# Queries and keys loaded with rows twice, low parts of probabilities in one operation a tile later, value blocks moved by 64

## The chip, the cores and the metric

The kernel runs on one core of a Trainium2 chip. The metric is the device time of one execution in microseconds (us). Before the change it is 1229.49 us, the median of three runs (1227.45 to 1229.86).

## What is computed

Attention with a threshold, then two feed-forward blocks, cut here to the arithmetic:

```python
# q, k, v: (4, 8, 576, 64), float32; tau = 0.02
scores = q @ k.T / 8
scores = where(scores >= rowmax(scores) - tau, scores, -1e9)
attn = exp(scores - rowmax(scores)); attn = attn / sum(attn)
x = (attn @ v).transpose(0, 2, 1, 3).reshape(2304, 512)
x = (silu(x @ w_gate) * (x @ w_val)) @ w_out      # 512 -> 1536 -> 512
x = (relu(x @ w_in) ** 2) @ w_out2                # 512 -> 2048 -> 512
```

All of it is float32; the weights reach the chip as 64-bit numbers. To keep the accuracy the kernel splits operands into a high part (rounded to the type in which PE multiplies) and a low part (the rest).

## The kernel before

**Tiles.** Attention is cut into 144 tiles of 128 query rows by 576 keys: 4 batches x 4 pairs of heads (NPAIR = 4) x 9 tiles. Of a pair's nine, A0 to A3 are the first head's rows 0 to 511, T is the last 64 rows of both heads together, and B2, B3, B0, B1 are the second head's. Tiles 0 to 35 are batch 0, tile 36 is the first of batch 1.

**A tile.** QK (L667, on PE) makes scores with the operands `qs` (rows 0 to 63 the high part of the scaled, transposed query, rows 64 to 127 its low part), `kh` (the high keys twice, one copy under the other) and `kl` (the low keys twice): two matmuls for each half of the columns give all four products of high and low. For tile T the operand is `qt`, in which the last 64 queries of each head have their own columns. RED (L677, DVE) takes the row maximum and subtracts tau, CUT (L685, ACT) applies the threshold, EXP (L693, ACT) the exponential with its row sum, RCP (L698, DVE) the reciprocal `r`. Then the two ways part:

- Batch 0: NORM on POOL, transposes on PE, copies `PH` on ACT and DVE, and value matmuls at L773.
- Batches 1 to 3 ("VV"): NORM on POOL makes `rs` (L706, one column, r times a constant) and the rounded high part of the probabilities in f16 (L707, into a buffer `both`). LO (L755, DVE) makes the low part, e x rs minus the high part, in two operations of 512 and 64 columns. XT (L761, a DMA on the SP queue) transposes high and low together, 9 blocks of 128 columns, into `pt`. AV (L780, PE) collects the tiles of one part of a head (there are four parts a pair, PARTS) and multiplies 14 times: 5 blocks of high probabilities and 4 of low ones by the high values `vs`, 5 blocks of high probabilities by the low values `v3`. The 576 high columns fill four blocks and a half, so the low ones begin in the middle of block 4: LO writes its last 64 columns there and its first 512 in blocks 5 to 8, and both use the same blocks of `vs`. ACT (L789) and DVE take the result out of PSUM.

**Preparing a pair.** `pair_steps` is a list of steps, one a tile, that runs through the tiles of the pair before. One load (`load_pair`, L472, SP queue) brings queries, keys and values of both heads, one head on rows 0 to 63, the other on 64 to 127, into `raw`, which has one buffer. Then come the rounded query (L612, ACT, into `land`), rounded keys (L70, ACT), low query (L618, DVE) and low keys (L78, POOL, two operations of 288 columns). `move` (L602) then copies each of the three to the rows where QK needs it, twice, by six SBUF-to-SBUF DMAs of half height a head on the SP queue. `tail` (L74, POOL) copies the last 64 queries into `qt`; for the T tile `kd` (L606) and `qd` (L608) are moved too. `values` splits the head's values out of the same `raw`: two copies (L74) and two subtractions, all on POOL. So `raw` is read until the next pair's own steps begin, and the next pair's load waits for the last reader.

**Fill.** Between tiles PE also works on the first feed-forward block for finished batches (`fill_group`: L258 and L300 matmuls); a credit in columns (`rate` 2600 a tile) sets how much. From about 541 us on the rest of the feed-forward blocks runs alone.

**Order.** The program names the steps in the order of the loop over `i` (the tile index): RED, CUT, EXP of tile i, then RCP, NORM, LO and XT of tile i - 1, QK of tile i + 1, fill, value matmuls of tiles `late` = 5 back, a step of `pair_steps`. A scheduler then orders each engine's instructions, with offsets (`early0`, `early`) that lift or lower steps. The engines and the SP queue run theirs strictly in order, and an instruction waits for semaphores at its place in the row.

```python
    both = [es[-1].bitcast(F16)[:, : 2 * S], *(ptp.tile(...) for j in range(2))]
            if i - 1 >= 9 * NPAIR:
                at_(LO, i - 1)
                at_(XT, i - 1)
```

The first line is of note: one of the three `both` buffers is the storage of the third `e` buffer, so in batches 1 to 3 EXP alternates between two.

Of the kernel before, what the change touches and what calls it, by code (L numbers as in the profile page):

```python
# [84 lines left out]
def attention_moe(tc, qkv, qk0, tau, w1, w2, out, cfg):  # L85
# [423 lines left out]

    def values(hd, h, raw):  # L510
# [11 lines left out]
        ops.sub(cfg["vl"], hd["v3"][:, :, :D], v, v2)  # L522

    def first_pair():

        raw = load_pair(0)
        for h in range(2):
            r = raw if h == 0 else rawp.tile([P, 2 * S], F32, name="raw01", tag="land")
            if h:
                for c in (0, S):  # L530
                    nc.sync.dma_start(r[:, c : c + S], qk0[h, :, c : c + S])
            else:

                for c in (slice(0, P), slice(S, 2 * S), slice(P, S)):
                    nc.sync.dma_start(r[:, c], qk0[h, :, c])
# [50 lines left out]
    def pair_steps(p):  # L586

        raw = load_pair(p)
        land = rawp.tile([P, 2, S], F32R, name=f"land{p}", tag="land")
        q, k = raw[:, 0:S], raw[:, S : 2 * S]  # L590
        qh, kh = land[:, 0], land[:, 1]

        def move(h):
            hd = head(h)
            rows = slice(hd["odd"] * D, (hd["odd"] + 1) * D)
            for dst, parts_ in (
                (hd["qs"], (qh, q.bitcast(F32R))),
                (hd["kh"], (kh, kh)),
                (hd["kl"], (k.bitcast(F32R), k.bitcast(F32R))),
            ):  # L600
                for j, src in enumerate(parts_):
                    nc.sync.dma_start(dst[j * D : (j + 1) * D, :].bitcast(F32), src[rows, :].bitcast(F32))  # L602
            tail(hd)
            if not hd["odd"]:
                hd["qd"], hd["kd"] = qds[0], qp.tile([P, S], F32R, name=f"kd{p}", tag="kd", bufs=1)
                nc.sync.dma_start(hd["kd"].bitcast(F32), k)  # L606
                for c in (slice(0, D), slice(D, P)):
                    nc.sync.dma_start(hd["qd"][c, c].bitcast(F32), qh[c, 4 * P : S].bitcast(F32))  # L608
# [1115 lines left out]
```

## Time and profile before

| | |
|---|---|
| median of 3 runs | 1229.49 us |
| the profiled execution, device time | 1229.54 us |
| its span in the trace | 1227.8 us |
| mean granted clock of TensorE | 0.968 |
| PE busy | 1113.4 us (91%), 6194 matmuls |
| DVE busy | 887.3 us (72%) |
| ACT busy | 615.1 us (50%) |
| POOL busy | 307.8 us (25%) |
| HBM read, written | 93.06 MB, 22.28 MB |

PE is TensorE's matmuls, PEld its weight loads, DVE VectorE, ACT ScalarE, POOL GpSimd, SP SyncE, whose queue (SPq) issues DMAs. Shares of busy time are of the whole span; attention with its fill takes the first 540 us, so a stage has to be looked at by itself. The granted clock is the share of TensorE's full 2.4 GHz that the chip allowed.

### The profile page before, as it was taken

The page shows a single profiled execution, that of the slowest core. Times are in us where ns is not written, and L with a number is a line of the kernel's source. Part 1 is how long each engine was busy: PE and PEld are TensorE (multiplying, and loading weights), DVE is VectorE, ACT ScalarE, POOL GpSimd, SP SyncE. Part 2 cuts the span into 40 slices and gives each one's busy share as a digit, 9 for nine tenths or more (in the row PEclk, how much of TensorE's full clock was granted, in tenths as well). Part 3 has the DMA queues.
Part 4 walks back from the last instruction along what each step waited for, and adds up shares of the span by engine and source line. Part 5 has one row for each costly group of instructions (what it writes and reads, how often), then busy time and mean ns, then how long its engine had stood idle before and what let it go on. Part 6 is the DMA issues. An engine that isn't in the chain of part 4 may idle for free.

```text
span 1227.8 us, 18958 instructions
## 1 busy us (share of the span) xinstructions
PE 1113.4 (91%) x6194; PEld 965.7 (79%) x6194; DVE 887.3 (72%) x2088; ACT 615.1 (50%) x1377; POOL 307.8 (25%) x524
## 2 busy tenths in 40 slices
PE   7998877667878877899999999999999999999998
PEld 6776766456667765799888888889889899889997
DVE  7888865765676757659998687878765858867554
ACT  7886644455554545535543343434555545554232
POOL 5577755654555646310000000000000000000000
PEclk9999988789989899999999999999999999999999
DMA  7768867777897787613222013436435444544452
GB/s 209 217 180 201 192 137 157 142 162 160 166 174 169 154 164 159 127 36 99 89 80 85 17 44 120 146 118 223 184 147 185 166 155 158 183 155 151 177 182 92
DMA packets 188258, 179.90 MB, mean 147 GB/s; under 512 B 138112, under 2 KB 139392, under 8 KB 188160
## 3 DMA queue, kind: packets, MB, share of 16 engines
q1 hardware_dynamic: 188016, 178.70, 54.4%
q8 instruction: 49, 0.80, 0.3%
q14 instruction: 49, 0.40, 0.1%
q10 hardware_dynamic: 144, 0.00, 0.0%
HBM read 93.06 MB, written 22.28 MB: 94 GB/s over the span
## 4 chain that ended last, share of the span: by engine, by line
PE 55%; POOL 14%; issue 9%; DMA 8%; DVE 8%; SPq 3%; ACT 3%; POOLq 0%; DVEq 0%; ACTq 0%
PE mm L258 16%; PE mm L1532 15%; PE mm L1479 11%; PE mm L300 7%; DMA raw<-in_qkv_dram 3%; POOL both L707 3%; POOL raw L78 3%; PE bank L258 2%; DMA qs<-raw 2%; POOL e L707 2%; DMA wr<-in_w_dram 2%; PE bank L780 1%; POOL vs L74 1%; POOL rs L706 1%; DVE st__114 L677 1%
## 5 line engine op out<-in xcount | busy, mean ns | idle before, releaser
L677 DVE TENSOR_SCALAR_CACHE_REDUCE st__114<-s,tau_c 128x576 bf16<-128x576 f32 x144 | 116.7, 811 | 36.8 <-PE s L667 25.9
L685 ACT ACTIVATE z<-s,thr 128x576 f32<-128x576 f32 x144 | 106.3, 738 | 48.9 <-DVE st__114 L677 40.6
L693 ACT ACTIVATE e<-z 128x577 f32<-128x577 f32 x144 | 98.5, 684 | 60.0 <-DVE r L698 38.8
L258 PE MATMUL mm<-xs,wa 128*128 128x512 f32 (+2 forms) x672 | 125.7, 347 | 0.5 <-ACT x L70 0.5
L258 PEld LDWEIGHTS mm<-xs,wa 128*128 128x128 f32 x672 | 109.4, 188 | 15.7 <-ACT x L70 0.7
L258 PE MATMUL bank<-xs_m,wa 128*128 128x288 f32 x576 | 100.2, 316 | 19.4 <-DVE xs_m L78 11.6
L780 PE MATMUL bank<-pt,vs 128*128 128x256 f16 (+1 forms) x432 | 76.5, 321 | 40.7 <-DMA pt<-both 21.2
L755 DVE SCALAR_TENSOR_TENSOR both<-e,rs,both 128x512 f16<-128x512 f32 (+1 forms) x144 | 85.6, 635 | 37.5 <-POOL both L707 37.2
L667 PE MATMUL s<-kh,qs 128*128 128x288 f32 x256 | 88.0, 361 | 24.9 <-ACT z L685 14.3
L258 PEld LDWEIGHTS bank<-xs_m,wa 128*128 128x128 f32 x576 | 86.2, 200 | 25.7 <-DVE xs_m L78 13.9
L780 PEld LDWEIGHTS <-vs 128*128 128x128 bf16 x432 | 41.2, 107 | 61.9 <-issue 28.4
L667 PEld LDWEIGHTS s<-kh,qs 128*128 128x128 f32 x256 | 50.5, 200 | 41.4 <-ACT z L685 26.0
L667 PE MATMUL s<-kl,qs 128*128 128x288 f32 x256 | 74.6, 312 | 3.7 <-DMA kl<-raw 3.7
L258 PE MATMUL mm<-xs,wb 128*128 128x512 f32 (+1 forms) x360 | 74.9, 368 | 0.0
L1549 DVE TENSOR_TENSOR xF<-xF,mm 128x512 f32<-128x512 f32 x54 | 36.9, 684 | 51.0 <-PE mm L1532 50.9
L258 PEld LDWEIGHTS mm<-xs,wb 128*128 128x128 f32 x360 | 62.8, 188 | 11.3
L755 DVE SCALAR_TENSOR_TENSOR e<-e,rs,e 128x512 f16<-128x512 f32 x72 | 47.2, 696 | 29.9 <-POOL e L707 29.8
L1532 PE MATMUL mm<-wb,wx 128*128 128x512 f32 x270 | 67.2, 389 | 0.0
L70 ACT ACTIVATE wb<-wf 128x256 fp32r<-128x256 f32 x82 | 34.0, 414 | 65.5 <-DVE wf L1134 38.4
L1479 PE MATMUL mm<-right,wb 128*128 128x384 f32 x348 | 65.3, 335 | 0.8 <-DVE right L78 0.8
L1131 ACT ACTIVATE wf<-wr 128x256 f32<-128x256 f32 x64 | 27.6, 433 | 69.6 <-DMA wr<-in_w_dram 49.3
L1479 PEld LDWEIGHTS mm<-right,wb 128*128 128x128 f32 x348 | 60.8, 188 | 1.5 <-DVE right L78 1.0
(163 smaller groups left out, 2645.7 us busy)
## 6 DMA issues: line engine op xcount, KB each, us to landing
wr<-in_w_dram SPq DMA_DIRECT2D x106, 256.0 KB, 3.0
raw<-in_qkv_dram SPq DMA_DIRECT2D x15, 896.0 KB, 5.9
kh<-land SPq DMA_DIRECT2D x60, 144.0 KB, 2.7
kl<-raw SPq DMA_DIRECT2D x60, 144.0 KB, 2.9
xF<-in_w_dram SPq DMA_DIRECT2D x30, 256.0 KB, 3.2
right<-kept1T SPq DMA_DIRECT2D x8, 768.0 KB, 5.5
right<-kept0T SPq DMA_DIRECT2D x7, 768.0 KB, 5.4
right<-kept SPq DMA_DIRECT2D x6, 768.0 KB, 4.3
```

Of the source, the lines that this page charges most:

```text
L258: mm(pt[:, :n], w[:, a, col + c * P : col + (c + 1) * P], xs[:, b, c, :], start=(i == 0), stop=(i == len(TERMS) - 1),)
L300: mm(pt[:, :n], ws[k][:, a, 2 * DM + m * P : 2 * DM + (m + 1) * P], us[k][:, b, :], start=(k == 0 and i == 0), stop=(k == ahead and i == 2),)
L667: mm(sp[:, cols], l, r[:, cols], start=(n_ == 0), stop=(n_ == len(pairs) - 1),)
L677: red = nc.vector.tensor_scalar(st_, st[t]["s"][:, :S], scalar1=tau_c, scalar2=None, op0=ALU.subtract, op1=ALU.max, accum_out=th)
L685: nc.scalar.activation(z[:, :S], st[t]["s"][:, :S], AF.Prelu, bias=st[t]["thr"], scale=-1.0, alpha=1 / SLOPE)
L693: ex = nc.scalar.activation(e, st[t]["z"], AF.Exp, scale=-SLOPE, accum_out=sum_)
L707: norm = nc.gpsimd.tensor_scalar(a[:, :S], e, scalar1=rs, scalar2=1.0, op0=ALU.mult, op1=ALU.mult)
L755: nc.vector.scalar_tensor_tensor(a[:, to : to + c.stop - c.start], e[:, c], r, a[:, c], op0=ALU.mult, op1=ALU.subtract)
L780: mm(o[:, :n], v, pt[:, k if k < 9 else k - 9, lo : lo + n], start=(k == 0), stop=(k == 13))
L1479: mm(bank[:, :BK], w[:, a, c * P : (c + 1) * P], t[:, b, c, :], start=(n == 0 and x in ("11", "12", "S1")), stop=(n == 5), skip_group_chec ...
L1532: mm(pt, u[:, b, s * P : (s + 1) * P], w[a], start=(half == 0 and j == 0 and i == 0), stop=(half == 1 and j == 1 and i == 2),)
L1549: nc.vector.tensor_tensor(acc[:, j, :], acc[:, j, :], pt, op=ALU.add)
```

## The change

**Queries and keys.** The input now holds each head's queries and keys with its 64 rows twice, so one load a head (`raw_head`, 128 x 1152, two buffers) lands them on all 128 rows. The rounded query and keys are computed at their place in `qs` and `kh`, the low query (64 rows) and the low keys too. `move`, `land`, `kd` and `qd` are gone. A pair has two query operations instead of one (on ACT; on POOL for pairs 1 to 3), two of keys (ACT), two low queries of 64 rows (DVE), four low-key operations (POOL) instead of two.

**Values.** They have a load of their own (`value_steps`): a pair's values are fetched at the seventh tile of the pair before and split at the pair's own tiles 3 and 5, the two copies on ACT instead of POOL. `vs` and `v3` have two buffers instead of three.

**Low parts.** LO is one operation of 576 columns that starts in the middle of block 4 and runs on, so the four low blocks hold keys shifted by 64 against the high ones. A second copy of the values, `vb`, shifted by 64 rows in the same way, is made of `vs` by two DMAs a head. LO and XT are issued one tile later, value matmuls too (`late` 6), `both` has three buffers of its own, and `rs` moves from POOL to DVE.

**Tile T** takes four pairs of factors (8 matmuls) instead of three (6).

```diff
@@ both, v3s, loads
-    both = [es[-1].bitcast(F16)[:, : 2 * S], *(ptp.tile([P, 2 * S], F16, name=f"both{j}", tag=f"both{j}") for j in range(2))]
-    v3s = [ptp.tile([P, 5, P], BF16, name=f"v3{j}", tag=f"v3{j}") for j in range(3)]
+    both = [ptp.tile([P, 2 * S], F16, name=f"both{j}", tag=f"both{j}") for j in range(3)]
+    v3s = [ptp.tile([P, 5, P], BF16, name=f"v3{j}", tag=f"v3{j}") for j in range(2)]
...
-    def load_pair(p):
-        raw = rawp.tile([P, RAWW], F32, name=f"raw{p}", tag="raw")
-        if p:
-            nc.sync.dma_start(raw, qkv[p])
-        return raw
+    def raw_head(h):
+        return rawp.tile([P, 2 * S], F32, name=f"raw{h}", tag=f"raw{h % 2}")
@@ values
-        vs = hd["vs"] = qp.tile([P, 5, P], BF16, name=f"vs{h}", tag="vs", bufs=3)
+        vs = hd["vs"] = qp.tile([P, 5, P], BF16, name=f"vs{h}", tag="vs", bufs=2)
...
         ops.sub(cfg["vl"], hd["v3"][:, :, :D], v, v2)
+        hd["vb"] = qp.tile([P, 4, P], BF16, name=f"vb{h}", tag="vb", bufs=2)
+        nc.sync.dma_start(hd["vb"][:D], vs[D:, :4])
+        nc.sync.dma_start(hd["vb"][D:], vs[:D, 1:])
@@ pair_steps (the old body is printed above)
+        raws = [raw_head(2 * p + j) for j in range(2)]
+
+        def query(j):
+            hd, q = head(2 * p + j), raws[j][:, :S]
+            if p < NPAIR:
+                nc.gpsimd.tensor_scalar(hd["qs"], q, scalar1=qscale, scalar2=1.0, op0=ALU.mult, op1=ALU.mult)
+            else:
+                nc.scalar.activation(hd["qs"], q, AF.Copy, scale=qscale)
+
+        def key(j):
+            hd, q = heads[2 * p + j], raws[j][:, :S]
+            ops.copy(cfg["kh"], hd["kh"], raws[j][:, S:])
+            low = hd["qs"][D:, :]
+            nc.vector.scalar_tensor_tensor(
+                low, q[D:, :], qscale[D:, :], low.bitcast(F32), op0=ALU.mult, op1=ALU.subtract
+            )
+
+        def key_low(j, c):
+            hd = heads[2 * p + j]
+            ops.sub(cfg["kl"], hd["kl"][:, c], raws[j][:, S:][:, c], hd["kh"][:, c].bitcast(F32))
+
+        halves_ = (slice(0, HS), slice(HS, S))
+        nc.sync.dma_start(raws[0], qk[2 * p])
         yield None
+        nc.sync.dma_start(raws[1], qk[2 * p + 1])
         yield None
+        query(0)
         yield None
+        key(0)
         yield None
+        key_low(0, halves_[0])
         yield None
+        key_low(0, halves_[1])
+        tail(heads[2 * p])
         yield None
+        if p < NPAIR:
+            values(heads[2 * p], 2 * p)
+        query(1)
         yield "next"
+        key(1)
+        key_low(1, halves_[0])
         yield None
+        key_low(1, halves_[1])
+        tail(heads[2 * p + 1])
+        if p < NPAIR:
+            values(heads[2 * p + 1], 2 * p + 1)
         yield None
+
+    def value_steps(i):
+        p, k = divmod(i, 9)
+        if k == 6 and NPAIR <= p + 1 < B * NPAIR:
+            rawv[p + 1] = rawp.tile([P, 2 * VW], F32, name=f"rawv{p + 1}", tag="rawv")
+            nc.sync.dma_start(rawv[p + 1], values_[p + 1])
+        if k in (3, 5) and NPAIR <= p < B * NPAIR:
+            h = 2 * p + (k == 5)
+            values(heads[h], h, rawv[p])
@@ QK, EXP, RCP, LO, AV
-            pairs = [(hd["qt"][:], hd[x_]) for hd in (ha, hb) for x_ in ("kh", "kl") if x_ == "kh" or "kd" not in ha]
-            if "kd" in ha:
-                pairs.append((ha["qd"], ha["kd"]))
+            pairs = [(hd["qt"][:], hd[x_]) for hd in (ha, hb) for x_ in ("kh", "kl")]
...
-        e = es[t % (len(es) if t < 9 * NPAIR else len(es) - 1)]
+        e = es[t % len(es)]
...
+        if way(t) == "VV":
+            rs = st[t]["rs"] = sm.tile([P, 1], F32, name=f"rs{t}", tag="rs")
+            nc.vector.tensor_scalar(rs, r, scalar1=UNIT, scalar2=None, op0=ALU.mult)
...
-        for to, c in ((S + D, slice(0, 4 * P)), (S, slice(4 * P, S))):
-            nc.vector.scalar_tensor_tensor(
-                a[:, to : to + c.stop - c.start], e[:, c], r, a[:, c], op0=ALU.mult, op1=ALU.subtract
-            )
+        nc.vector.scalar_tensor_tensor(a[:, S:], e[:, :S], r, a[:, :S], op0=ALU.mult, op1=ALU.subtract)
...
-                v = hd["vs"][:, (0, 1, 2, 3, 4, 0, 1, 2, 3)[k], :] if k < 9 else hd["v3"][:, k - 9, :]
+                v = hd["vs"][:, k, :] if k < 5 else hd["vb"][:, k - 5, :] if k < 9 else hd["v3"][:, k - 9, :]
@@ the loop over i
-            if i - 1 >= 9 * NPAIR:
-                at_(LO, i - 1)
-                at_(XT, i - 1)
+        if 9 * NPAIR <= i - 2 < NTILE:
+            at_(LO, i - 2)
+            at_(XT, i - 2)
...
+            at_(value_steps, i, name="PS")
@@ the input and CFG
+    q, k = (x.reshape(B * H, S, D).transpose(0, 2, 1) for x in (q, k))
+    qk = np.concatenate([np.concatenate([x, x], axis=1) for x in (q, k)], axis=2)
...
-    full[NPAIR:, D:, :, 4] = full[NPAIR:, :D, :, 4]
+    full[NPAIR:, D:, :, 4] = full[NPAIR:, :D, :, 0]
...
-    "vh": "P",
+    "vh": "A",
-    "late": 5,
+    "late": 6,
```

**How the order moves.** First the SP queue at the end of batch 2, where pair 11's queries and keys are moved and pair 12's are loaded. Before (`raw_3423` and `land_3425` belong to pair 11, `qs_3711` and so on to its second head, `raw_3791` is pair 12's load):

```order
L606 DMA kd_3625<-raw_3423 128x576
L608 DMA qd_136<-land_3425 64x64 x2
L761 DMA_TRANSPOSE pt<-e_104 128x9x128
L602 DMA qs_3711<-land_3425 64x576
L602 DMA qs_3711<-raw_3423 64x576
L602 DMA kh_3712<-land_3425 64x576 x2
L602 DMA kl_3713<-raw_3423 64x576
L761 DMA_TRANSPOSE pt<-both_106 128x9x128
L602 DMA kl_3713<-raw_3423 64x576
L761 DMA_TRANSPOSE pt<-both_107 128x9x128
L761 DMA_TRANSPOSE pt<-e_104 128x9x128
L472 DMA raw_3791<-in_qkv_dram 128x1792
```

The same queue in the changed kernel (`raw_3293` is the load of pair 11's second head, `raw_3662` that of pair 12's first, `vs` and `vb` are values of pair 10):

```order
L609 DMA raw_3293<-in_qk_dram 128x1152
L768 DMA_TRANSPOSE pt<-both_108 128x9x128
L768 DMA_TRANSPOSE pt<-both_106 128x9x128
L768 DMA_TRANSPOSE pt<-both_107 128x9x128
L519 DMA vb_3348<-vs_3343 64x512
L520 DMA vb_3348<-vs_3343 64x512
L768 DMA_TRANSPOSE pt<-both_108 128x9x128
L607 DMA raw_3662<-in_qk_dram 128x1152
L768 DMA_TRANSPOSE pt<-both_106 128x9x128
L768 DMA_TRANSPOSE pt<-both_107 128x9x128
```

Between the transposes there are only loads and the two copies into `vb`; no row of the queue waits for ACT, DVE or POOL to have split queries or keys.

Second, ACT at the head of the program: the first keys, the first query, then CUT (L685 before, L693 after) and EXP (L693, L701) of tiles 0 and 1. Before:

```order
L70 ACTIVATE kh_150<-raw_142 128x288 x2
L571 ACTIVATE qs_149<-raw_142,qscale 128x448
L685 ACTIVATE z_105<-s_121,thr_166 128x576
L693 ACTIVATE e_102,sum_169<-z_105 128x577
L685 ACTIVATE z_105<-s_122,thr_175 128x576
```

After:

```order
L69 ACTIVATE kh_148<-raw_140 128x288 x2
L568 ACTIVATE qs_147<-raw_140,qscale 128x448
L69 ACTIVATE vs_1214<-rawv_1038 128x5x64
L69 ACTIVATE vs_1306<-rawv_1038 128x5x64
L693 ACTIVATE z_105<-s_120,thr_164 128x576
L69 ACTIVATE vs_1214<-rawv_1038 128x5x64
L701 ACTIVATE e_102,sum_167<-z_105 128x577
L69 ACTIVATE vs_1306<-rawv_1038 128x5x64
L693 ACTIVATE z_105<-s_121,thr_173 128x576
```

The four copies of pair 4's values (used from tile 36 on) stand among the first two tiles' operations.

Third, DVE in the middle of the attention stage: RED (L677 before, L685 after), LO (L755, L764), RCP (L698, L706) and, after, `rs` (L709) and the low query (L598). Before:

```order
L698 RECIPROCAL r_3384<-sum_3343 128x1
L677 TENSOR_SCALAR st__114,thr_3426<-s_122,tau_c 128x576
L755 SCALAR_TENSOR_TENSOR both_107<-e_103,rs_3386,both_107 128x512
L755 SCALAR_TENSOR_TENSOR both_107<-e_103,rs_3386,both_107 128x64
L698 RECIPROCAL r_3433<-sum_3381 128x1
L677 TENSOR_SCALAR st__114,thr_3465<-s_121,tau_c 128x576
L755 SCALAR_TENSOR_TENSOR e_104<-e_102,rs_3435,e_104 128x512
L755 SCALAR_TENSOR_TENSOR e_104<-e_102,rs_3435,e_104 128x64
```

After:

```order
L685 TENSOR_SCALAR st__113,thr_3295<-s_121,tau_c 128x576
L764 SCALAR_TENSOR_TENSOR both_108<-e_103,rs_3267,both_108 128x576
L706 RECIPROCAL r_3301<-sum_3263 128x1
L598 SCALAR_TENSOR_TENSOR qs_3387<-raw_3292,qscale,qs_3387 64x576
L709 TENSOR_SCALAR rs_3303<-r_3301 128x1
...
L685 TENSOR_SCALAR st__113,thr_3352<-s_120,tau_c 128x576
L764 SCALAR_TENSOR_TENSOR both_106<-e_104,rs_3303,both_106 128x576
```

A tile's LO stands one RED behind its RCP before and after alike (`r_3384`, `thr_3426`, LO with `rs_3386`; `r_3301`, `thr_3352`, LO with `rs_3303`); what is new in the row is `rs` on DVE and one operation in the place of two.

## Rows read from the trace of the kernel before

**Rows 1.** Busy us by stretch: PE, PEld, DVE, ACT, POOL (count), clock, DMA share, GB/s

```profile
27.00:91.83 64.83, 59.80 (x360) 50.97 (x359) 55.12 (x147) 56.34 (x131) 40.83 (x58) 1.00 0.71 197
91.83:492.57 400.74, 308.14 (x1920) 253.61 (x1919) 279.47 (x656) 209.60 (x470) 234.99 (x397) 0.90 0.80 164
541.10:1200.00 658.90, 657.22 (x3378) 582.97 (x3379) 494.50 (x1142) 300.43 (x669) 0.00 (x0) 1.00 0.40 137
500.00:513.00 13.00, 10.46 (x71) 8.55 (x72) 10.18 (x29) 9.60 (x21) 5.50 (x13) 1.00 0.77 138
```

**Rows 2.** Timeline of DVE, line 677: start, duration, operation, [wait and releaser]

```profile
91.83 0.81 DVE L677 TENSOR_SCALAR_CACHE_REDUCE st__114<-s,tau_c 128x576 bf16<-128x576 f32 x1
...
269.29 0.82 DVE L677 TENSOR_SCALAR_CACHE_REDUCE st__114<-s,tau_c 128x576 bf16<-128x576 f32 x1
...
284.53 0.82 DVE L677 TENSOR_SCALAR_CACHE_REDUCE st__114<-s,tau_c 128x576 bf16<-128x576 f32 x1 [5.13 <-PE s L667]
...
289.20 0.82 DVE L677 TENSOR_SCALAR_CACHE_REDUCE st__114<-s,tau_c 128x576 bf16<-128x576 f32 x1 [0.70 <-ACT e L693]
...
291.30 0.82 DVE L677 TENSOR_SCALAR_CACHE_REDUCE st__114<-s,tau_c 128x576 bf16<-128x576 f32 x1 [0.34 <-issue]
...
492.57 0.82 DVE L677 TENSOR_SCALAR_CACHE_REDUCE st__114<-s,tau_c 128x576 bf16<-128x576 f32 x1 [0.66 <-PE s L667]
```

**Rows 3.** Timeline of POOL and of the SP queue at tiles 80 and 81

```profile
267.10 2.01 POOL L78 TENSOR_TENSOR raw<-raw,land 128x288 fp32r<-128x288 f32 x2
...
280.18 1.26 SPq L602 DMA_DIRECT2D kl<-raw  x2
...
287.84 0.24 POOL L74 TENSOR_SCALAR qt<-qs 128x64 fp32r<-128x64 f32 x1 [9.11 <-DMA qs<-raw]
...
292.41 0.47 SPq L472 DMA_DIRECT2D raw<-in_qkv_dram  x1
```

**Rows 4.** Waits, 91.83 to 492.57: waiter <- releaser: us in all, times, longest

```profile
ACT xF L789 <- PE bank L780: 54.7, 22, 8.4
POOL qt L74 <- DMA qs<-raw: 45.7, 8, 9.1
```

**Rows 5.** Groups by form, 91.83 to 492.57: busy us, mean ns | idle before

```profile
L755 DVE SCALAR_TENSOR_TENSOR both<-e,rs,both 128x512 f16<-128x512 f32 x66 | 56.6, 857 | 34.5 <-POOL both L707 34.2
L755 DVE SCALAR_TENSOR_TENSOR both<-e,rs,both 128x64 f16<-128x64 f32 x66 | 28.0, 424 | 0.0
L74 POOL TENSOR_SCALAR vs<-raw 128x320 bf16<-128x320 f32 x44 | 23.0, 523 | 14.3 <-DMA raw<-in_qkv_dram 12.2 <-PE bank L780 1.1
L698 DVE RECIPROCAL r<-sum 128x1 f32<-128x1 f32 x100 | 15.5, 155 | 3.2 <-ACT e L693 3.0
L618 DVE SCALAR_TENSOR_TENSOR raw<-raw,qscale,land 128x576 fp32r<-128x576 f32 x11 | 10.8, 980 | 4.1 <-ACT land L612 4.1
L612 ACT ACTIVATE land<-raw,qscale 128x576 fp32r<-128x576 f32 x11 | 8.5, 773 | 7.7 <-DMA raw<-in_qkv_dram 7.0 <-issue 0.6
```

**Rows 6.** A dense run of PE in the chain that ended last: start, us, releaser

```profile
521.41 11.20 PE bank L258 x84
```

**Rows 7.** Start of the program: timeline of SP queue and ACT, then DMA issues

```profile
7.23 0.33 SPq L472 DMA_DIRECT2D raw<-in_qkv_dram  x1
...
8.07 0.74 ACT L685 ACTIVATE z<-s,thr 128x576 f32<-128x576 f32 x1 [2.43 <-DVE st__114 L677]
...
raw<-in_qkv_dram SPq DMA_DIRECT2D x15, 896.0 KB, 5.9
x<-in_qkv_dram SPq DMA_DIRECT2D x8, 160.0 KB, 3.5
```

**Rows 8.** Timeline of DVE: LO while POOL subtracts low keys, and later

```profile
267.17 2.02 DVE L755 SCALAR_TENSOR_TENSOR e<-e,rs,e 128x512 f16<-128x512 f32 x2 [0.62 <-POOL e L707]
...
289.95 0.94 DVE L755 SCALAR_TENSOR_TENSOR both<-e,rs,both 128x512 f16<-128x512 f32 x2
```

More of the change, by code (lines that the diff above doesn't have):

```diff
@@ L82, in split, with attention_moe @@
         self.sub(elo, lo, src, hi.bitcast(F32))
-def attention_moe(tc, qkv, qk0, tau, w1, w2, out, cfg):
+def attention_moe(tc, qk, values_, tau, w1, w2, out, cfg):
     nc = tc.nc
@@ L506, in whole_values, with values @@
             c0 += hd["odd"] * D
-            a = 2 * S + hd["odd"] * VW
-            nc.sync.dma_start(flat[:, c0 : c0 + VW], qkv[h // 2, :, a : a + VW])
-    def values(hd, h, raw):
+            a = hd["odd"] * VW
+            nc.sync.dma_start(flat[:, c0 : c0 + VW], values_[h // 2, :, a : a + VW])
+    def values(hd, h, raw=None):
         odd = hd["odd"]
@@ L522, in values @@
         ops.sub(cfg["vl"], hd["v3"][:, :, :D], v, v2)
+        hd["vb"] = qp.tile([P, 4, P], BF16, name=f"vb{h}", tag="vb", bufs=2)
+        nc.sync.dma_start(hd["vb"][:D], vs[D:, :4])
+        nc.sync.dma_start(hd["vb"][D:], vs[:D, 1:])
     def first_pair():
[L526 removed]
         for h in range(2):
[L528 removed]
+            r = raw_head(h)
             if h:
                 for c in (0, S):
[L531 removed]
+                    nc.sync.dma_start(r[:, c : c + S], qk[h, :, c : c + S])
             else:
                 for c in (slice(0, P), slice(S, 2 * S), slice(P, S)):
[L535 removed]
+                    nc.sync.dma_start(r[:, c], qk[h, :, c])
                 nc.vector.tensor_scalar(qscale, tau_t, scalar1=0.0, scalar2=0.125, op0=ALU.is_ge, op1=ALU.mult)
@@ L579, in s2 @@
                 tail(hd)
-                values(hd, h, raw)
+                values(hd, h)
             yield s0
@@ L586, in pair_steps @@
     def pair_steps(p):
[L588 to L608, printed above, removed]
+        raws = [raw_head(2 * p + j) for j in range(2)]
@@ L625, in pair_steps @@
-        move(2 * p)
+        key_low(0, halves_[1])
+        tail(heads[2 * p])
         yield None
-        values(heads[2 * p], 2 * p, raw)
+        if p < NPAIR:
+            values(heads[2 * p], 2 * p)
+        query(1)
         yield "next"
-        move(2 * p + 1)
+        key(1)
+        key_low(1, halves_[0])
         yield None
-        values(heads[2 * p + 1], 2 * p + 1, raw)
+        key_low(1, halves_[1])
+        tail(heads[2 * p + 1])
+        if p < NPAIR:
+            values(heads[2 * p + 1], 2 * p + 1)
@@ L704, in NORM @@
             a = st[t]["both"] = both[(t + 1) % len(both)]
-            rs = st[t]["rs"] = sm.tile([P, 1], F32, name=f"rs{t}", tag="rs")
-            nc.gpsimd.tensor_scalar(rs, r, scalar1=UNIT, scalar2=1.0, op0=ALU.mult, op1=ALU.mult)
+            rs = st[t]["rs"]
             norm = nc.gpsimd.tensor_scalar(a[:, :S], e, scalar1=rs, scalar2=1.0, op0=ALU.mult, op1=ALU.mult)
@@ L951, in attention_moe @@
             at_(av_parts, 3, name="AV")
-        if i == 4:
-            with tc.issue_after(st[2]["norm"]):
-                for x_ in qds:
-                    nc.gpsimd.memset(x_.bitcast(F32), 0.0)
         at_(mp1.flush, "P", name="FP")
@@ L1657, in pack @@
     return [
-        ("in_qkv_dram", np.ascontiguousarray(qkv)),
-        ("in_qk0_dram", np.stack([np.concatenate([qkv[0, r : r + D, : 2 * S]] * 2) for r in (0, D)])),
+        ("in_qk_dram", np.ascontiguousarray(qk)),
+        ("in_v_dram", full.reshape(B * NPAIR, P, 2 * VW)),
         ("in_tau_dram", np.ascontiguousarray(tau)),
```

23 lines of the change are left out of this document (4 added, 19 removed).

## The prediction

> **What bounds the kernel now.** I read the stages first, from the busy time by stretch [rows 1]. Its columns give, for each engine, busy microseconds, and then granted clock and share of the DMA engines. From 541 us on PE has hardly a gap (657 of 659 us up to 1200), and the change touches nothing there. Tiles 0 to 35 (batch 0) end at 91.8 us; from 27 us on PE is busy 92% of the time (59.80 of 64.83), DVE 85%, ACT 87%. The weak stretch lies between the row maxima of tile 36 (91.83) and tile 135 (492.57): 400.74 us for eleven head pairs, **36.4 us a pair**, with PE at 77%, DVE at 70%, and a granted clock of 0.90, so part of it ran at the lower of the two levels.
>
> Next, the rhythm in it: the times of L677, the first operation of a tile on DVE [rows 2]. Within a pair tiles follow each other every 2.2 us or so (289.20 to 291.30), but tile 81, the first of a pair, starts at 284.53 after DVE had stood idle for QK's matmuls; the tile before it had started at 269.29. From pair 6 to pair 15 the step to a pair's first tile is 9.8 to 22.2 us, ten of ten. Eight steps of 2.2 us make 17.6 of the 36.4; the rest is the boundary.
>
> Then the cause, from the waits and the SP queue. At that boundary POOL had the low keys ready at 269.1; SP moved them to their rows at 280.18, behind the transposes in its queue, and moved the odd head's after them; POOL itself stood 9.11 us at `tail` for moved queries, with the NORMs of the next tiles behind it; and the next pair's load went out only at 292.41, since its one buffer had to be read out first [rows 3]. Over the stretch POOL lost 45.7 us to those query moves, and ACT 54.7 us to value matmuls that came late [rows 4]. So the boundary is a serial chain, load, split, move, QK, across four engines and one queue.
>
> **The change, part by part.**
>
> *Moves and the late load.* Twelve half-height moves, kd and two qd a pair go. In the new SP order no step of the query and key path stands on SP but the two loads, and these stand some nine tiles ahead of the operations that read them. The chain of the boundary then has no transfer left in it, and a pair costs what its busiest engine needs. So I price a pair by each engine, from the eleven-pair sums [rows 1] and durations of one operation [rows 5].
>
> - PE: 1920 recorded matmuls, 174.5 a pair, plus 2 (a T tile now has four pairs of factors instead of three). Dense, 84 of them took 11.20 us, 0.133 each [rows 6], so 176.5 x 0.133 = 23.5 us. At batch 0's 92% that is 25.6. At the busy time it has now, 28.0 + 0.3 over 0.92, it is 30.8: that would be with the clock no better than 0.90.
> - DVE: 279.47/11 = 25.4 us. LO's two operations take 857 + 424 = 1.28 us a tile; the one of 576 columns is nearest to L618 (two f32 inputs, 576 columns, mean 0.98), so 9 x 0.30 = 2.7 us go. `rs` comes over from POOL: 9 x 0.155 = 1.4 (price of L698, also one column). The low queries are 2 x 0.98 instead of one: +1.0. Together 25.1 us. At batch 0's 85% this is **29.5 us**; at PE's 92% it would be 27.3.
> - ACT: 209.60/11 = 19.1 us, plus one query and one key operation (0.77 each at most), plus four value copies (0.52 each at most, their price on POOL): 22.7, or 26.1 at 87%.
> - POOL: 234.99/11 = 21.4 us, less four value copies (2.1) plus two more low-key operations (2 x 1.0, [rows 3]): 21.3 before the nine `rs` are taken off. No bound.
> - DMA engines: 0.80 x 36.4 = 29.1 us a pair. Between 500 and 513 us hardly anything but transposes ran: 13 us at 138 GB/s, six of 0.295 MB each, in 13 x 0.77 us, so 1.65 us each and 14.9 a pair. The other 14.2 us carried 0.92 MB of loads and 2.1 MB of moves (and 0.3 of weights): 4.3 us per MB. Now it is 1.18 MB of queries and keys, 0.33 of values and 0.26 of `vb`: 7.6 us, and 1.2 for weights. Together 23.7 us, under DVE, though at 29 us a pair the engines are as full as before.
>
> I take **29 us a pair**, between the two DVE values and nearer to batch 0's, since the rhythm of that stage is the nearest this trace has to a stretch without boundaries. Eleven pairs: 11 x (36.4 - 29) = **-81 us**. The ends are 25.6 (PE dense, clock full), -119, and 32 (the 30.8 of an unimproved clock and about a microsecond of new waits), -48.
>
> *LO and XT one tile later.* On DVE nothing moves by that: LO of a tile stood one RED behind its reciprocal and stands so still. What goes is the passage to POOL for `rs`: LO into `both` lost 34.2 us to NORM, 0.52 each time [rows 5], and some of it may go. That is inside the 29 us. AV also comes one tile later, so the transpose has the same four tiles of lead.
>
> *Values.* Pair 4's value load and copies now stand at the head of the program: ACT has two of them ahead of the very first CUT. Before, that CUT ran at 8.07. The value load takes the place on SP where pair 1's load stood (7.23), and carries 320 KB; 160 KB took 3.5 us and 896 KB 5.9 [rows 7]. So it lands between 10.7 and 13.1, and with two copies (0.5 each) CUT starts at 11.7 to 14.1: +3.6 to +6.0, **+5** taken. It is paid once, and nothing runs beside it yet. Two `vb` transfers a head are in the DMA sum; what reads them comes four tiles later.
>
> *Batch 0.* Pairs 1 to 3 lose their moves, but POOL gets two query operations and two more low-key ones each, 3.5 us beside its 63%. I take **0**, with -4 (if their boundaries gain too) to +5.
>
> *The end.* After the last QK 272 matmuls are left in the program instead of 229 (one value part and some output groups of the fill more): up to 43 x 0.133 = 5.7 us, **+3** taken, 0 if the tiles hide them.
>
> Sum: 1229.5 (this execution; its span is 1227.8, and the median of the three runs is the same 1229.5) - 81 + 5 + 0 + 3 = **1156 us**, with ends 1229.5 - 119 + 3.6 - 4 = 1110 and 1229.5 - 48 + 6 + 5 + 5.7 = 1198.
>
> **Rivals.**
>
> *PE is the only bound* (25.6 us a pair): 1229.5 - 119 + 8 = 1118. For it: in the new order QK alternates with 12 or 14 other matmuls, so PE always has a group ready. Against: DVE would need 98%.
>
> *POOL slows DVE.* Beside low-key operations on POOL, one LO pair took 2.02 us; with POOL free, 0.94 [rows 8]. The stretch's mean of 1.28 means that about 3 of 9 are hit. The change has two more such POOL operations a pair and packs everything closer. If five or six are hit, DVE needs 2.4 us more: (25.1 + 2.4)/0.85 = 32.4 a pair, 1229.5 - 44 + 8 = 1193. This is also where a page speaks against the change. The Trainium skill, GPSIMD Engine Reference, section Specifications, says that GpSimd shares its SBUF interfaces with VectorE, and that instructions of VectorE with two SBUF inputs contend; LO is such an instruction and stays one. The trace agrees; by that rule alone the time would be nearer 1193 than 1156.
>
> *Slower: the values take over as the boundary.* The place is ACT, which works in order. `vs` has two buffers instead of three, and ACT now writes it, twice a pair, waiting for the value matmuls of the same buffer; its second copy waits for POOL, whose subtraction waits for ACT's first. CUT and EXP of all later tiles stand behind. Such waits of ACT for value matmuls exist now: 22 of them, 2.5 us in the mean, 8.4 at the longest [rows 4]. Two a pair on the path cost 5 us at the mean: 34 a pair, 1211. From 3.35 us each the gain is gone (2 x 3.35 = 7.4 - 8/11); at 4.5 with the same 8 us at both ends it is 29 + 9 = 38 a pair, 1229.5 + 18 + 8 = 1255. Against: the long waits stand at today's boundaries, where value matmuls pile up, and these should go.
>
> *No change.* If the loads do not run ahead in practice (SP stuck on an earlier wait), the boundary stays and gain and start-up cost nearly cancel: 1227 to 1232.
>
> **How the numbers follow.** Forecast (27.5 to 31 us a pair, 1134 to 1178): 0.52. PE dense, 1118: 0.12. POOL against DVE, or waits of that size, 1193, reaching to 1211: 0.23. Slower, 1255: 0.09. No change: 0.04. The range 1115 to 1200 takes in the first two and most of the third, and leaves out the slower case, the unchanged one and the third's upper tail, some 0.18. About 0.2% is what a measurement can tell from no change here; faster by more than that 0.87, within it 0.04, slower 0.09.
>
> **What would show it.** Right: steps of L677 within 2 to 5 us throughout from tile 36 on and a pair at 27.5 to 31 us; no wait of POOL for a DMA at `tail`; PE and DVE both above 80% there and a granted clock above 0.95; the first CUT at 12 to 14 us; DMA share still near 0.8. Wrong: steps of 8 us and more left at pair boundaries, with ACT waiting at `vs` for value matmuls or SP waiting at a load; LO of 576 columns at 1.3 us or more; QK or AV waiting for transposes that land late behind the 590 KB loads; or batch 0 ending after 100 us.

## The result

The changed kernel takes **1160.68 us** (median of 4 runs, 1160.34 to 1161.5) against 1229.67 (median of 4, 1227.45 to 1230.52): ratio 0.9443, 95% interval 0.9426 to 0.9459. Forecast was 1156, range 1115 to 1200. The profiled execution took 1160.94 us, span 1159.1, mean granted clock 0.99.

Busy time of the changed kernel by stretch, columns as in [rows 1]; the stretches are batch 0 without its start, tile 36 to tile 135, and the feed-forward stage:

```profile
27.00:100.18 73.18, 69.03 (x410) 57.83 (x410) 69.14 (x175) 67.20 (x161) 55.52 (x75) 1.00 0.40 130
100.18:412.90 312.72, 266.69 (x1870) 234.26 (x1868) 264.68 (x647) 225.99 (x511) 207.89 (x263) 0.97 0.77 157
470.00:1130.00 660.00, 657.89 (x3390) 584.22 (x3390) 492.97 (x1141) 299.74 (x669) 0.00 (x0) 1.00 0.40 136
```

The stretch of eleven pairs fell from 400.74 to 312.72 us, from 36.4 to **28.4 us a pair**; PE, DVE and ACT are each busy more of it (85%, 85%, 72%), the clock rose from 0.90 to 0.97. PE stands idle 46.0 us of it instead of 92.6, and its busy time fell by 41.5, with 1870 recorded matmuls at 0.143 us instead of 1920 at 0.160. So nearly half of the 88 us lies in PE's busy time: some 8 for the 50 matmuls fewer, the rest in shorter matmuls, with the higher clock beside them. Whether the clock is a cause of the shorter pair or only follows from it, no run shows. The feed-forward stage is as it was.

The timeline of DVE shows where the boundary went. These are RED of tiles 36, 79, 80, 81, 82, 135 and 143 (now line 685); they answer to [rows 2]:

```profile
100.18 0.80 DVE L685 TENSOR_SCALAR_CACHE_REDUCE st__113<-s,tau_c 128x576 bf16<-128x576 f32 x1
...
229.86 0.82 DVE L685 TENSOR_SCALAR_CACHE_REDUCE st__113<-s,tau_c 128x576 bf16<-128x576 f32 x1
232.76 0.79 DVE L685 TENSOR_SCALAR_CACHE_REDUCE st__113<-s,tau_c 128x576 bf16<-128x576 f32 x1
236.69 0.82 DVE L685 TENSOR_SCALAR_CACHE_REDUCE st__113<-s,tau_c 128x576 bf16<-128x576 f32 x1
238.71 0.81 DVE L685 TENSOR_SCALAR_CACHE_REDUCE st__113<-s,tau_c 128x576 bf16<-128x576 f32 x1
...
412.94 0.80 DVE L685 TENSOR_SCALAR_CACHE_REDUCE st__113<-s,tau_c 128x576 bf16<-128x576 f32 x1
...
437.16 0.82 DVE L685 TENSOR_SCALAR_CACHE_REDUCE st__113<-s,tau_c 128x576 bf16<-128x576 f32 x1
```

From tile 80 to 81 it is 3.9 us now, 15.2 before; the longest step of the stretch is 6.5. In the mean of the eleven pairs the step to a pair's first tile fell from 15.2 to 4.4 us, but each of the other eight rose from 2.7 to 3.0: of the 10.7 us that a boundary lost, 2.7 came back within the pair.

The sum over the stages, from the two profiled executions (1229.54 to 1160.94, -68.6): tile 36 starts at 100.18 and not at 91.83, **+8.4**; the eleven pairs, 312.76 for 400.74 by RED of tiles 36 and 135, **-88.0**; tiles 135 to 143 take 24.2 us for 17.7 (RED of the two stood at 492.57 and 510.3 before), **+6.5**; from the last RED to the end of the span 721.9 for 717.5, **+4.4**.

What waits in the stretch (waiter <- releaser: us in all, times, longest):

```profile
PEld s L675 <- ACT z L693: 39.7, 33, 4.0
ACT z L693 <- DVE st__113 L685: 36.9, 29, 4.2
DVE both L764 <- POOL both L717: 36.4, 49, 2.2
PE s L675 <- ACT z L693: 34.1, 29, 3.7
POOL both L717 <- DVE rs L709: 24.6, 21, 2.3
...
ACT vs L69 <- POOL rawv L77: 8.0, 11, 1.8
```

The largest wait for a DMA is 2.4 us in all (NORM, for a transpose that still reads `both`). The 45.7 us of POOL at `tail` and the 54.7 of ACT for value matmuls [rows 4] are gone; what is left are waits of DVE, ACT, POOL and PE for each other within a tile.

### The profile page after: what moved, and what is told of

It is laid out like the page before. It is cut to its first block, busy times and chain, and to the rows that moved or that the text cites. A ratio compares the mean times of both kernels' runs of the same rounds, so it can differ in the third digit from the quotient of the medians.

```text
span 1159.1 us, 18607 instructions
## 1 busy us (share of the span) xinstructions
PE 1085.5 (94%) x6224; PEld 958.6 (83%) x6224; DVE 886.2 (76%) x2103; ACT 640.3 (55%) x1449; POOL 300.1 (26%) x402
## 4 chain that ended last, share of the span: by engine, by line
PE 61%; DVE 3%; POOL 1%; issue 1%; ACT 1%; POOLq 0%; ACTq 0%
PE mm L257 18%; PE mm L1536 17%; PE mm L1483 14%; PE mm L299 9%; PE bank L257 1%; PE bank L299 1%; PE bank L787 1%; DVE st__113 L685 0%; POOL both L717 0%; DVE right L77 0%; DVE sum L1369 0%; ACT z L693 0%; DVE both L764 0%; DVE h L1470 0%; DVE wa L77 0%
## 5 line engine op out<-in xcount | busy, mean ns | idle before, releaser
L693 ACT ACTIVATE z<-s,thr 128x576 f32<-128x576 f32 x144 | 106.1, 737 | 77.0 <-DVE st__113 L685 42.5
L764 DVE SCALAR_TENSOR_TENSOR both<-e,rs,both 128x576 f16<-128x576 f32 x108 | 108.1, 1003 | 42.5 <-POOL both L717 41.7
L685 DVE TENSOR_SCALAR_CACHE_REDUCE st__113<-s,tau_c 128x576 bf16<-128x576 f32 x144 | 116.3, 808 | 10.3 <-ACT vs L69 5.8
L717 POOL TENSOR_SCALAR both<-e,rs 128x576 f16<-128x576 f32 x108 | 87.5, 812 | 69.0 <-DVE rs L709 26.9
L257 PE MATMUL bank<-xs_m,wa 128*128 128x288 f32 x576 | 93.0, 309 | 8.8 <-DVE xs_m L77 3.7
L701 ACT ACTIVATE e<-z 128x577 f32<-128x577 f32 x144 | 98.4, 683 | 4.1 <-DVE both L764 0.3
L1553 DVE TENSOR_TENSOR xF<-xF,mm 128x512 f32<-128x512 f32 x54 | 36.9, 684 | 51.0 <-PE mm L1536 51.0
L1470 DVE TENSOR_TENSOR h<-mm,h 128x384 f32<-128x384 f32 x72 | 39.6, 551 | 30.4 <-PE mm L1483 30.4
L77 POOL TENSOR_TENSOR kl<-raw,kh 128x288 fp32r<-128x288 f32 x62 | 60.4, 991 | 5.9 <-ACT kh L69 5.9
```

What stands on the lines that cost most here:

```text
L77: e.tensor_tensor(out, a, b, op=ALU.subtract)
L257: mm(pt[:, :n], w[:, a, col + c * P : col + (c + 1) * P], xs[:, b, c, :], start=(i == 0), stop=(i == len(TERMS) - 1),)
L685: red = nc.vector.tensor_scalar(st_, st[t]["s"][:, :S], scalar1=tau_c, scalar2=None, op0=ALU.subtract, op1=ALU.max, accum_out=th)
L693: nc.scalar.activation(z[:, :S], st[t]["s"][:, :S], AF.Prelu, bias=st[t]["thr"], scale=-1.0, alpha=1 / SLOPE)
L701: ex = nc.scalar.activation(e, st[t]["z"], AF.Exp, scale=-SLOPE, accum_out=sum_)
L717: norm = nc.gpsimd.tensor_scalar(a[:, :S], e, scalar1=rs, scalar2=1.0, op0=ALU.mult, op1=ALU.mult)
```

## The experiments

Times are medians; differences are to the changed kernel's 1160.7 where nothing else is said. The kernel before ran beside every group, with medians of 1229.3 to 1230.6; the changed kernel was not run again, so a difference of about 1 us to it says little. Edits are cut to what matters; `...` and the remarks behind `#` stand for the rest.

### First group: the two halves alone, the start, LO

**loads_alone**: the changed kernel with the low parts as they were.

```diff
+        for to, c in ((S + D, slice(0, 4 * P)), (S, slice(4 * P, S))): ...   # LO in two
+            nc.gpsimd.tensor_scalar(rs, r, ...)                              # rs on POOL
+                at_(LO, i - 1); at_(XT, i - 1)
+    "late": 5,   # no vb, both[0] in e[2], three vs and v3
```

> The changed kernel with the low parts as before: LO in two operations on tile i - 1, no vb, rs on POOL, late 5, two e buffers in batches 1 to 3, three vs and v3 buffers. Theory (the serial chain load, split, move, QK was the boundary): nearly the whole gain stays. DVE gets 9 x 0.27 us for LO back and loses 9 x 0.15 of rs, 1.1 us a pair, at 85% busy 1.3 us, for 12 pairs 16 us: 1177 us, 1165 to 1190, and no step of RED above 8 us at a pair's first tile. Rival (buffers, one LO and the later XT gave half of it or more): 1195 us or more.

Measured: 1188.8 us, ratio to before 0.9662 (0.9644 to 0.968). The boundary steps are gone (the step to a pair's first tile is 5.8 us at the longest), so the theory's mark holds; its time just does too, within 1165 to 1190, but at the upper end: 28 us dearer than the changed kernel, where 16 were worked out. So not "nearly the whole gain" stays, but 42 us of 70. Its waits in tiles 36 to 135 show one that the price of `rs` had not contained, POOL's for the reciprocal:

```profile
POOL rs L711 <- DVE r L703: 57.6, 53, 2.2
```

**lowparts_alone**: the kernel before with the low parts of the changed one, moves and `load_pair` kept.

```diff
+        nc.vector.scalar_tensor_tensor(a[:, S:], e[:, :S], r, a[:, :S], ...)
+            nc.vector.tensor_scalar(rs, r, scalar1=UNIT, ...)
+            at_(LO, i - 2); at_(XT, i - 2)     # vb, late 6, three both; T tile without qd, kd
```

> The kernel before with the low parts of the changed one (one LO a tile later, vb, rs on DVE, late 6, three e and both buffers, two vs) and its T tile of four pairs of factors, so kd and qd go; load_pair, raw and the twelve moves a pair stay. Theory: the boundary stays, steps of 8 to 20 us at pairs' first tiles: 1220 us, 1205 to 1232. Rival: 1195 us or less.

Measured: 1223.0, ratio 0.9941 (0.992 to 0.9962). The boundary stays: the steps to the first tiles of pairs 6 to 15 are 13.1 to 20.0 us. Of 70 us, 42 come from the loads alone and 7 from the low parts alone: 21 appear only when both stand. That a cheaper tile only reaches the same boundary sooner would explain it, but is not shown.

**start_late**: pair 4's four value copies are taken out of the program's head.

```diff
+            with tc.issue_after(st[i - 4]["exp"]) if p == NPAIR else nullcontext():
                 values(heads[h], h, rawv[p])
```

> The changed kernel, but pair 4's four value copies on ACT queue behind EXP of tiles 35 and 37 instead of standing ahead of the first CUT. Theory (they cost the start 5.7 us, once): first CUT at about 8.1 us, tile 36 some 6 us earlier, 1155 us (1152 to 1157). Rival (the delay is taken up later, or the copies cost as much at batch 1's start): 1160 to 1162 us.

Measured: 1159.7 (1159.2 to 1160.1). In the changed kernel the first CUT indeed waits for the copies and the load in front of them, from 8.07 [rows 7] to 13.77 (timeline of ACT):

```profile
13.04 0.83 ACT L69 ACTIVATE vs<-rawv 128x320 bf16<-128x320 f32 x2 [7.27 <-DMA rawv<-in_v_dram]
13.77 0.72 ACT L693 ACTIVATE z<-s,thr 128x576 f32<-128x576 f32 x1
```

Without them CUT starts at 8.25, and tiles 2 and 3 at 10.4 and 12.1, within 0.2 us of the kernel before; but then NORM stands behind a query of pair 1 on POOL, which waits for its load (timeline of POOL in start_late):

```profile
14.04 0.74 POOL L590 TENSOR_SCALAR qs<-raw,qscale 128x576 fp32r<-128x576 f32 x1 [2.96 <-DMA raw<-in_qk_dram]
14.75 2.07 POOL L77 TENSOR_TENSOR kl<-raw,kh 128x288 fp32r<-128x288 f32 x2
16.80 0.74 POOL L721 TENSOR_SCALAR e<-e,r 128x576 f32<-128x576 f32 x1
```

So tile 36 comes only 2.7 us earlier (97.5), 5.7 behind the kernel before, and the stretch after it is 2.3 us longer (315.0). The time lies just below the rival's 1160 to 1162 and well above the theory's 1152 to 1157: the start has two causes, one behind the other, and taking out the first alone gives little.

**lo_two_ops**: `for c in (slice(0, 4 * P), slice(4 * P, S))` around LO.

> The changed kernel with LO in two operations of 512 and 64 columns to the same places; nothing else. If DVE sets the pair (24.1 us busy of 28.4): 9 x 0.27 = 2.4 us more at 85% are 2.9 us a pair, 12 pairs 34 us: 1190 to 1198 us. If PE sets it, with DVE's gaps free: 1160 to 1167 us.

Measured: 1167.2, +6.5, at the upper edge of the 1160 to 1167 that were expected if DVE does not set the pair. Its busy time in the stretch:

```profile
99.60:420.20 320.60, 273.56 (x1870) 238.46 (x1868) 289.31 (x743) 226.84 (x511) 204.89 (x261) 0.96 0.77 153
```

DVE got 24.6 us more work (289.31 for 264.68) and the stretch grew by 7.9: two thirds went into gaps. DVE's busy time alone does not set the pair.

### Second group: which part of the low parts, which part of the loads

**rs_on_pool**: `rs` computed by `nc.gpsimd.tensor_scalar` ahead of NORM.

> The changed kernel with rs back on POOL, ahead of NORM. The runs so far: the loads alone gave 42 us of 70, the low parts alone 7, so 21 come only where both stand. Theory 1 (each VV tile is a loop DVE, POOL, DVE, and rs on DVE took one hand-over out of it): +8 to +16 us, 1169 to 1177, POOL waiting for the reciprocal some 60 us in the stretch. Theory 2 (the third e buffer gave it): 1158 to 1164 us, as DVE loses 1.3 us a pair of work.

Measured: 1176.1, **+15.4**. DVE has 6 us less work (258.40 for 264.68) and the stretch is 15.3 longer:

```profile
99.90:427.90 328.00, 277.79 (x1870) 242.26 (x1868) 258.40 (x549) 225.77 (x511) 226.76 (x359) 0.93 0.74 150
```

```profile
DVE both L762 <- POOL both L715: 57.7, 61, 2.6
POOL rs L714 <- DVE r L706: 44.4, 38, 2.8
```

These are lines of its windows and of its waits. LO's wait for NORM went from 36.4 to 57.7 us, and POOL waited 44.4 for the reciprocal, where theory 1 had some 60. Less work on DVE, a slower kernel, by the size that theory 1 gave. Its reason, a hand-over taken out, does not hold: wherever `rs` is made, a tile passes from DVE to POOL and back to DVE once (RCP, `rs`, NORM, LO). What differs is that on POOL `rs` takes longer and stands straight ahead of NORM (groups of rs_on_pool and of the changed kernel):

```profile
L714 POOL TENSOR_SCALAR rs<-r 128x1 f32<-128x1 f32 x98 | 27.0, 276 | 47.5 <-DVE r L706 44.4 <-ACT z L693 1.4 <-ACT qs L592 0.8
...
L709 DVE TENSOR_SCALAR rs<-r 128x1 f32<-128x1 f32 x98 | 14.5, 148 | 1.3
```

The granted clock fell too, to 0.93 from 0.97, and PE was busy 11.1 us longer for the same 1870 matmuls. How much of the 15 us is the longer way of a tile and how much the clock, no run separates.

**two_e_buffers**: `both = [es[-1].bitcast(F16)..., *2 tiles]`, EXP between two, LO and XT on i - 1, late 5.

> The changed kernel with the third both in the storage of the third e, EXP between two e buffers in batches 1 to 3, LO and XT on tile i - 1, late 5. Theory 2 (EXP waits for LO of two tiles back, which the third buffer ended): +10 to +18 us, 1171 to 1179, EXP waiting for LO 20 us or more in the stretch. Theory 1 (the hand-over of rs): within 4 us of 1161.

Measured: 1164.1, +3.4, so theory 2 falls. With 15.4 of `rs` and 6.5 of LO that is 25.3 of the 28 by which loads_alone was dearer; these three parts add up.

**kl_moved**: low keys written in `raw`, then two half-height DMAs a head into `kl`.

> The changed kernel, but the low keys are written in place in raw and brought to kl by two half-height moves a head on the SP queue, as before for that part alone. Theory A (a move behind the transposes of the SP queue lengthens the chain of a pair's start): steps of RED of 8 us and more at pairs' first tiles again, +15 to +40 us, 1176 to 1200. Theory B (the load that came late was the cause; a move of a split that is ready two tiles ahead is hidden): within 5 us of 1161.

Measured: 1163.3, +2.6. **one_raw_buffer**: `tag=f"raw{h % 2 if h < 2 * NPAIR else 0}"`.

> The changed kernel with one raw buffer for both heads from batch 1 on, so a head's load waits for the last reader of the other's, as load_pair did; no moves. Theory B (the late load): steps of 8 us and more, at B tiles or at first tiles, +10 to +40 us, 1171 to 1200. Theory A (the moves): within 5 us of 1161.

Measured: 1162.2, +1.5. Each theory had its part of the chain down for 10 us or more, and neither part alone brings the boundary back. In kl_moved a pair's first load still goes out 36.9 us ahead of its first tile (mean of pairs 7 to 15; 42.0 in the changed kernel), in one_raw_buffer 27.0. There the second head's load is 13.2 us ahead of the first tile, but tile T, the fifth, is the first that reads it.

### Third group: the moves, and what bounds the tiles now

**moves_kept**: lowparts_alone with the values out of `raw`, in the load and at the tiles of the changed kernel.

```diff
-        raw = rawp.tile([P, RAWW], ...)      # loaded with values
+        raw = rawp.tile([P, 2 * S], ...)     # and value_steps, "vh": "A"
```

> The run lowparts_alone (1223 us), with the values out of raw: they have a load of their own and are split at the pair's tiles 3 and 5 with copies on ACT, as in the changed kernel; so raw is free for the next load as soon as the moves have read it. The twelve moves a pair stay. It differs from the changed kernel by rows loaded once, one raw and the moves. Theory A (the moves, behind transposes and behind each other on the SP queue): steps of 8 us and more at pairs' first tiles stay, 1195 to 1223 us. Theory B (the load that waited for the value split): 1165 to 1175 us.

Measured: 1177.7, between the theories and nearer to B: 45 us of the way from 1223 without any move taken out, and 17 left for the moves, the one `raw` and rows loaded once. The first tiles of pairs 6 to 15 still come with steps of 10.9 to 14.6 us.

**moves_kept_copies_on_pool**: the same with `"vh": "P"`.

> The run moves_kept (1177.7 us) with the four value copies a pair back on POOL; values still have a load of their own. lowparts_alone, with values in raw and their copies on POOL, took 1223. Theory B (the load that waited for the value split was worth the 45 us between them): 1176 to 1190 us. Rival C (POOL's value copies in front of NORM, and PE waiting for split values, 97 us of PE waits in lowparts_alone, were worth it): 1200 to 1223 us.

Measured: 1183.9, within theory B's range and far from rival C's. So 39 of the 45 us come from the values leaving `raw` (with the place of their split and of the copies into `vb`), 6 from ACT copying them. The timelines show what that changed. In lowparts_alone: load of pair 9, first tile of pair 9, load of pair 10 (SP queue, DVE, SP queue):

```profile
248.88 0.53 SPq L472 DMA_DIRECT2D raw<-in_qkv_dram  x1
...
269.39 0.82 DVE L673 TENSOR_SCALAR_CACHE_REDUCE st__113<-s,tau_c 128x576 bf16<-128x576 f32 x1 [1.77 <-PE s L663]
...
282.11 0.53 SPq L472 DMA_DIRECT2D raw<-in_qkv_dram  x1
```

and in moves_kept_copies_on_pool, load and first tile of pair 10, load of pair 11:

```profile
259.78 0.52 SPq L473 DMA_DIRECT2D raw<-in_qkv_dram  x1
...
282.62 0.82 DVE L687 TENSOR_SCALAR_CACHE_REDUCE st__113<-s,tau_c 128x576 bf16<-128x576 f32 x1 [0.35 <-PE s L677]
...
290.15 0.52 SPq L473 DMA_DIRECT2D raw<-in_qkv_dram  x1
```

With one `raw` a pair's load goes out behind the first tile of the pair before it, whose moves have still to read the buffer: 8.8 to 12.7 us behind it in lowparts_alone (loads of pairs 7 to 15), 7.3 to 8.8 in moves_kept_copies_on_pool. From the load to the pair's own first tile it takes 24.5 and 23.6 us in the mean. The two parts make up a pair: 35.3 and 31.7 us (in the kernel before 26.6 + 9.3 = 35.8). That they add up is no proof, it holds in any kernel; what counts is the sign of the part behind the first tile. In the changed kernel the load of pair 9's first head goes out at 197.76, 39 us ahead of its first tile at 236.69 and ahead of pair 8's at 214.44 too, and the second head's at 212.60. The part behind the first tile is negative, -13.2 us in the mean of pairs 7 to 15, and the ring load, split, moves, first tile, next load is open:

```profile
197.76 0.34 SPq L607 DMA_DIRECT2D raw<-in_qk_dram  x1
212.60 0.33 SPq L609 DMA_DIRECT2D raw<-in_qk_dram  x1
```

Of the 3.6 us between the two kernels with one `raw`, 2.7 lie behind the first tile. There, in lowparts_alone, the value split of the second head had still to read `raw`, but it ended 0.4 to 7.7 us ahead of the load (4.0 in the mean), and SP stood at these nine loads for hardly any time: each went out 0.1 to 0.2 us behind the row ahead of it in the queue, a transpose or a copy into `vb`. At the copies SP had waited for the split and for value matmuls (8.1 us in all in moves_kept_copies_on_pool):

```profile
SPq L524 <- POOL vs L74: 18.3, 10, 3.9
SPq L524 <- PE bank L775: 13.0, 7, 5.6
```

So what held the load as the kernel ran was its place in a queue that works in order; that the split's reading of `raw` held it is not shown.

**norm_takes_r**: `scalar1=r, scalar2=UNIT` in NORM.

> The changed kernel, NORM multiplies by r and by the constant itself, so it waits for the reciprocal and not for rs; rs stays on DVE for LO alone. rs on POOL cost 15 us. If the hand-over DVE to POOL in each tile still sets the pace (POOL waited 25 us for rs in the stretch): 1152 to 1158 us. If what is left is set elsewhere (PE with its fill, CUT): 1159 to 1162 us.

Measured: 1161.2, no change. NORM loses as much to the reciprocal as it did to `rs` (24.6), and now also waits for transposes that still read its buffer of `both` (2.4 in the changed kernel):

```profile
POOL both L716 <- DVE r L706: 29.2, 20, 3.5
POOL both L716 <- DMA pt<-both: 23.2, 13, 3.0
```

A shorter way from RCP to NORM gave nothing, so this hand-over does not set the pace by itself.

**fill_rate_3000**: `"rate": 3000`.

> The changed kernel with 3000 columns of fill a tile instead of 2600, so that less of it is left after the last tile. If the tiles' hand-overs set the pair and PE has room (24.2 us busy of 28.4): up to 6 us less at the end, 1154 to 1158 us. If PE sets the pair, the same work only moves: 1159 to 1163 us.

Measured: 1163.8, +3.1. Tile 135 starts 13.1 us later (426.0) and the end follows its start by 735.3 us in place of 746.2 (spans 1161.3 and 1159.1): work put between the tiles lengthens them by a little more than the 10.9 us it saves behind. PE, busy 85%, takes no more for nothing; the granted clock of the stretch is 0.94 there, 0.97 in the changed kernel.

No run beats the changed kernel by more than start_late's 1 us.

## Why the prediction was right, step by step

- **The boundary and its chain.** Right. Every kernel with one `raw` and the moves keeps the large steps. They are gone with neither, and also with the one `raw` alone or the moves of the low keys alone. The share of the links was not foreseen: the prediction spoke of moves behind transposes first, and of the load last; most (39 us) came with the values leaving `raw`, 17 with the moves, the one `raw` and the single rows. The reason for the late load at 292.41, "its one buffer had to be read out first", is too simple as well. POOL's split had ended at 278.73; the last moves then read `raw`, and a transpose stood ahead of the load (POOL, then the SP queue of the kernel before):

```profile
277.63 1.10 POOL L78 TENSOR_TENSOR v<-raw,vs 128x320 bf16<-128x320 f32 x1
...
286.84 1.24 SPq L602 DMA_DIRECT2D kl<-raw  x2
290.95 1.28 SPq L761 DMA_TRANSPOSE pt<-both  x1
```

- **Steps of 2.2 us within a pair.** They are the median of the 88 steps, the mean is 2.7. So of 36.4 us the eight steps took 21.3 and the boundary 15.2, not 17.6 and 18.8; and the steps did not stay as they were, but rose to 3.0.
- **29 us a pair** (28.4 measured). The size was right, partly by luck: the price was not derived from what sets it. DVE's 25.1 us at batch 0's 85% were measured as 24.1 at 85%; yet in the experiments 24.6 us more work on DVE cost the stretch only 7.9, and 6 less cost 15. So the busy share is no constant of DVE that a work sum can be divided by; batch 0's happened to be met. What does set the pair, the waits within a tile, PE with its clock, or both, is not shown. The term "`rs` comes over from POOL: +1.4 us a pair" had the wrong sign: the kernel without it is 15.4 us slower, 1.3 a pair over twelve.
- **LO as one operation**: it took 1.01 us in the mean (98 times in the stretch) where 0.98 was priced, but in lo_two_ops 2.2 us more of DVE's work a pair cost 0.7 us a pair.
- **Values, +5.** The first CUT came 5.7 us later, inside the bounds; batch 0 then lost 2.7 more, where 0 was taken. That it is "paid once" at that place is not the whole of it: with the copies away, 5.7 of the 8.4 us stay, and NORM stands behind POOL's query.
- **The end, +3**: 4.4 measured. **Missed** was tiles 135 to 143, +6.5: the sum took eleven pairs at the new length and left the last one at its old one. These eight steps have no boundary among them and so nothing to gain, but they too went from 2.2 to 3.0 us each; the granted clock there was 0.86, and 1.00 before. So the total came out within 5 us partly because a gain of 88 for 81 met losses of 19 for 8.
- **Rivals.** PE dense at 25.6 did not come (clock 0.97, waits for CUT). Values as a new boundary did not: ACT lost 8.0 us to POOL's subtraction there, with 1.8 the longest. POOL slowing DVE is real but smaller, below.
- **The signs.** Busy shares, clock, DMA share (0.77), `tail` and the first CUT came as named. The steps of 2 to 5 us did only in 71 of 99 cases: 19 were shorter, 9 longer, up to 6.5. One sign of being wrong was met: batch 0 ended after 100 us, at 100.18, and the time still came out near the forecast.

What stays open: whether values outside `raw` gained through the smaller load, the place of the split, or the transposes and `vb` copies that stood ahead of the load in the SP queue. 2.7 of the 3.6 us lie behind the first tile, which speaks against the smaller load as the main part, but no run has one alone. All twelve moves with two `raw` buffers were not tried either. lowparts_alone also has two `vs` buffers with the split on POOL, and PE waited 46.1 us there for split values, so its 7 us may be too low.

## What to carry to other kernels

Where a single buffer is loaded, split, moved and read, look whether the next load goes out before or after the first use of this one, and what stands ahead of it in its queue: here, taking the values out of that buffer was worth 39 to 45 us, while cheaper tiles with the late load brought only 7. Once the boundary is gone, an engine's busy time does not give the price of an operation: one on the busier engine can be the cheaper choice (15 us here). Removing a boundary also gives back less than its own length (8.0 of 10.7 us a pair here), since the tiles between take longer. The two halves of this change were not additive (42 and 7 of 70 us), so each part has to be tried with the others in place.

## What was not expected of the hardware

LO of 576 columns has two durations. Of 92 single rows in the stretch, 47 overlap a two-input subtraction on POOL (line 77) by over 0.1 us and take 1.17 us in the mean, the other 45 take 0.83. The Trainium skill, GPSIMD Engine Reference, section Specifications, has the two engines contend for their SBUF interfaces; the trace agrees, with 0.34 us a meeting. The prediction had 1.08 us for two operations from one pair of rows [rows 8]: about half meet, 4.6 of nine for the rival's five or six, and each costs a third.

The starts and ends of the rows that meet say how. Two meetings, each with LO and POOL's subtraction:

```profile
402.92 1.35 DVE L764 SCALAR_TENSOR_TENSOR both<-e,rs,both 128x576 f16<-128x576 f32 x1 [0.31 <-POOL both L717]
402.85 0.81 POOL L77 TENSOR_TENSOR m_u<-m_th,m_u 128x288 fp32r<-128x288 f32 x1
...
203.20 0.89 DVE L764 SCALAR_TENSOR_TENSOR both<-e,rs,both 128x576 f16<-128x576 f32 x1
203.56 1.18 POOL L77 TENSOR_TENSOR m_u<-m_th,m_u 128x288 fp32r<-128x288 f32 x1
```

In the first POOL began earlier and took 0.81 us, and LO ended 0.61 us after it; in the second LO began earlier, and POOL ended 0.65 us after LO. Of 28 meetings of single rows that POOL began, LO ended 0.60 to 0.66 us after POOL in every one; of 11 that LO began, POOL ended 0.65 to 0.68 us after LO. So in these rows one of the two operations waits for the end of the other, and the price of a meeting is what is left of the one that began first.
